# Two attention kinds and a gated MLP on one core: chunks in natural order, and a schedule planner that models shared load bandwidth

## The chip, the cores and the metric

The kernel runs on one core of one Trainium2 chip. The metric is the device time of one execution in microseconds, as the median of several runs. Beside it stands one execution under the hardware profiler, from which the profile's numbers come; its times are microseconds from the start of the span.

## The reference, cut to what matters

Attention over 4 batches of 8 heads, 768 positions of 64 values. Heads 0, 2 and 6 see all earlier positions ("full" heads); the other five see the first 4 positions and a window of 64 ("stream" heads). What comes out, all heads side by side (3072 x 512), goes through two weight matrices with a gate between them.

```
scores = scale * np.matmul(q, k.transpose(0, 1, 3, 2))
stream_keep = causal & (is_sink | in_win)          # 4 sinks, window 64
mask = causal for full heads, stream_keep for the others
a = softmax(scores where mask)
x = (a @ v) with the heads side by side            # 3072 x 512
h = x @ w_in                                       # 512 x 2048
g = h * (1.0 / (1.0 + np.exp(-beta * h)))
out = g @ w_out                                    # 2048 x 512
```

## The kernel before

The work is cut into eight chunks: one batch and one half (384 positions) of its sequence each. For a chunk, four pairs of heads (p and p + 4, one in the upper and one in the lower 64 rows of TensorE) go through scores (task S), exp on ScalarE, a mask, the product with the values (PV), and the division by the row sum on VectorE (rec, x). A chunk that is the second half of its batch also needs the first half's keys and values: a full head has 15 blocks of 128 x 128 scores there instead of 6, a stream head 6 instead of 5. The chunk's x is transposed (Tx on TensorE with an eviction, or Xx by a DMA), and then come 16 groups F1 of four matmuls with w_in (line 701), each followed by a tanh on ScalarE (703) and a gate product on VectorE (705), and 12 groups F2 of four matmuls with w_out (719), whose results are scaled into osb tiles (730, 732) and stored from the SP queue (735). F1.1.3 below is the fourth F1 group of chunk 1; F2.0.0.4 is chunk 0, first 128 rows, gate blocks 4 to 7.

Keys and queries reach TensorE in two ways. In the way of the ramp (`load_pair`, `keys_ramp`) float32 pairs are loaded from SP, cast, transposed by TensorE (Tk, Tq, line 448) and evicted. In the way of rows (`load_rows`, `keys_rows`) GpSimd issues DMAs that cast to bfloat16 (417), twelve to a chunk, and SP issues DMA transposes (462) into KT and QT. Before, chunks 0, 1 and 2 go the first way (`N_F32 = 3`). Values are loaded from SP (`load_v`, 392) into four vs tiles and copied to VX (CV) and, for the stream heads' previous block and sinks, to VO; KO holds the like for keys. The first two chunks add their masks on TensorE (M, line 590); later ones multiply on VectorE. Four PSUM banks are for scores (`S_BANKS`) and four for all else (`G_BANKS`).

The weights come in four parts each, issued by GpSimd. `W_AFTER` names for each part a load that must have landed first: GpSimd copies one element of it (`held`), then issues the DMA.

The order on every engine is written by a planner (`Plan.run`) when the kernel is built. It plays the tasks through with estimated durations and puts each task where its engine is first free; on chip each engine runs its list in that order and waits where an operand isn't there yet. `pick` chooses among tasks that are ready: on TensorE attention always stands ahead of F1 and F2. A transfer's landing is estimated with one common queue:

```
begin = max(dma_free, now + occ + 1000.0)
dma_free = begin + service
t.done = dma_free + 1000.0
```

`fill` puts matmuls on zeros into planned holes of the first 36 us.

Of the kernel before, what the change touches and what calls it, by code (L numbers as in the profile page):

```python
# [16 lines left out]
class Slots:  # L17


    def __init__(self, names, in_turn=False):  # L20
        self.names = list(names)
        self.free = [0.0] * len(self.names)
        self.in_turn, self.holds = in_turn, []
# [5 lines left out]
    def turn(self, hold):  # L29
        if not self.in_turn:  # L30
            return True
        while self.holds and self.holds[0].got is not None:
            self.holds.pop(0)
        return self.holds[0] is hold
# [41 lines left out]
class Plan:  # L76


    SEM = {"PE": 55.0, "ACT": 40.0, "DVE": 38.0, "POOL": 66.0, "SP": 70.0}
    SWITCH = 100.0  # L80

# [10 lines left out]
    def run(self, pick):  # L92
# [7 lines left out]
        def enter(t):  # L100
            for e, occ, lat in t.alts:
                at = max((d.start if e == d.engine == "PE" else d.done + self.SEM[e] for d in t.deps), default=0.0)
                at = max([at] + [d.start for d in t.follow])
                ready[e].append((at, t, occ, lat))
# [5 lines left out]
        dma_free = 0.0  # L110
        lanes = {"hw": [], "sw": []}
        n = len(self.tasks)
        left = n
        while left:
# [72 lines left out]
RAMP_C = 2  # L187
FILL_END, FILL_SPARE = 36000.0, 120.0
N_F32 = 3
W_AFTER = [("v", 0, 0), ("q", 1, 3), ("v", 1, 0), ("v", 1, 2), ("wi", 1), ("wi", 2), ("wo", 0), ("wo", 1)]  # L190
C2_AFTER = ("wi", 2)
V2_AFTER = ("wi", 3)


def XT_PE(c, m):
    return c < 4 or (c == 7 and m % 2)
# [3 lines left out]
def kernel(  # L200
# [24 lines left out]
    chunks = [(b0 + i, h2) for b0 in range(0, B, 2) for h2 in range(2) for i in range(2)]  # L225
# [47 lines left out]
    A7 = sb([128, 5, 128], BF16, "A7")  # L273
    Ac = sb([128, 5, 128], BF16, "Ac")
    junk = sb([1, 64], F32, "junk")
# [49 lines left out]
    t_as = ops("DVE", 100, [lambda: less(A7[:, 0:3], M7[:, 0:3]), lambda: nc.vector.tensor_copy(out=A7[:, 3:5], in_=A7[:, 1:3])], "adds", [t_m, t_m1, t_m2], prio=-24)  # L325
# [18 lines left out]
    seq = [0]  # L344

    def dma(name, queue, issue, service, deps, fn, take=(), drop=(), prio=None, follow=()):
        seq[0] += 1
        kind = "sw" if queue == "POOL" else "hw"
        lat = 0.0
        return P.add(name, [(queue, issue, lat)], deps, seq[0] * 0.001 + (prio or 0), lambda _: fn(eng[queue]), take, drop, land=(kind, service), follow=follow)  # L350
# [45 lines left out]
    def load_w_in(i, key):  # L396
        f = slice(i * 512, (i + 1) * 512)
        t = held(key, lambda: w_in_sb[0:1, 0, i * 512:i * 512 + 1])
# [3 lines left out]
    def load_w_out(i, key):  # L402
        f = slice(i * 4, (i + 1) * 4)
        t = held(key, lambda: w_out_sb[0:1, i * 4, 0:1])
# [5 lines left out]
    def load_rows(c, deps=(), follow=()):  # L410
        b, h2 = chunks[c]
        hold = Hold(stage_r)
        for name, src in (("k", k), ("q", q)):
            i = "kq".index(name)
            for t in range(HT):
                r = h2 * HALF + t * 128
                ROW[name, c, t] = [dma(f"row{name}{c}.{t}.{a}", "POOL", 750, 850, list(deps), lambda e, t=t, a=a, r=r, i=i, src=src: e.dma_start(  # L417
# [38 lines left out]
    def keys_rows(c, deps=()):  # L456
        hold = ROW[c]
        for name, holder, made in (("k", KH, GK), ("q", QH, GQ)):
            i = "kq".index(name)
            ts = []  # L460
            for t in range(HT):
                ts.append(dma(f"X{name}{c}.{t}", "SP", 1250, 650, ROW[name, c, t] + list(deps), lambda e, t=t, i=i, holder=holder: e.dma_start_transpose(
# [5 lines left out]
    def sinks(c):  # L468
# [3 lines left out]
        for p in OP:  # L472
# [8 lines left out]
            for src, lo, hi, at in todo:  # L481
                ts.append(P.add(f"KO{c}.{p}", [dve((hi - lo) * 128, 0.27), pool((hi - lo) * 128)], GK[src, p], c * 100 + 50 + p,
# [3 lines left out]
            t = P.add(f"KOs{c}.{p}", [dve(16), pool(16, 4.0)], ts + GK[f, p], c * 100 + 50 + p,  # L486
# [4 lines left out]
    def values(c):  # L491
# [3 lines left out]
        for t in range(HT):  # L495
            hold = LD["vhold", c, t]
            GV[c].append(P.add(f"CV{c}.{t}", [pool(512, 0.96), dve(512, 0.53)] if c >= 2 else [dve(512, 0.53), act(512, 20)], [LD["v", c, t]], c * 100 + 60,
# [4 lines left out]
        on = (lambda n: [dve(n, 0.27)]) if c < RAMP_C else (lambda n: [pool(n, 0.9), dve(n, 0.27)])  # L502
# [13 lines left out]
    def side_of(c, p, a):  # L516
# [7 lines left out]
        if retr[h]:  # L524
# [14 lines left out]
            return bks, per, [("c", (0, 1))], 16 if h2 else 7  # L539
# [3 lines left out]
        for i in range(HT):  # L543
# [4 lines left out]
            else:  # L548
                at = i - 1 if h2 == 0 else i
                order.append((K(c, i - 1) if c < RAMP_C else KOk(at), VOv(at), i))  # L550
# [10 lines left out]
    def attention(c, p):  # L561
# [13 lines left out]
        for rs in groups:  # L575
# [4 lines left out]
            m_task = []  # L580
            if by_pe:
                def put(_, work=work):
                    for a, r, bank in work:
                        lo, lst = sides[a][0][r]
                        w = sum(n for _, _, n in lst)
                        if sides[a][2][0][0] == "s":
                            add = A7[:, lo:lo + w].rearrange("p k j -> p (k j)")
                        else:
                            add = Ac[:, 2 * r:2 * r + 3].rearrange("p k j -> p (k j)")
                        nc.tensor.matmul(bank.buf[:, 0:add.shape[1]], ident, add, start=True, stop=False)  # L590
                m_task = [P.add(f"M{c}.{p}", [pe(384 * len(work), len(work))], [t_ac, t_as, t_id], prio + 1, put, take=[w[2] for w in work])]

            def go(_, work=work):
# [7 lines left out]
                for r, at, a, kk, q0, n, bank in sorted(todo, key=lambda x: x[:3]):  # L601
                    to, of = bank.buf[:, at * 128:(at + n) * 128], QH[c].buf[half(a), p, q0 * 128:(q0 + n) * 128]
                    nc.tensor.matmul(to, kk(), of, start=not by_pe, stop=(r, at + n) == ends[a, r] or not by_pe)  # L603
                if by_pe:
                    for a, r, bank in work:
                        if sides[a][2][0][0] == "s" and r == 1:
                            nc.tensor.matmul(bank.buf[0:sink_i, 0:128], sink_of(c, a, p), QH[c].buf[half(a), p, 256:384], start=True, stop=True)
# [66 lines left out]
    def x_transposed(c):  # L674
        for m in range(MO):
# [11 lines left out]
            else:  # L687
                XTD[c, m] = dma(f"Xx{c}.{m}", "SP", 1250, 480, deps, lambda e, m=m: e.dma_start_transpose(
# [66 lines left out]
    for i in range(4):  # L755
        load_w_in(i, W_AFTER[i])
# [3 lines left out]
    for i in range(4):  # L760
# [104 lines left out]
```

## Time and profile before

| | before |
|---|---|
| median of 3 runs | 235.78 us (235.77 to 235.97) |
| the profiled execution | 237.91 us, of which span 236.1 us |
| mean granted TensorE clock | 0.993 |
| instructions in the span | 5174 |
| read from and written to memory | 27.27 MB, 6.29 MB |

Busy times are shares of the span. A matmul's end is modelled, so TensorE's busy time is over what it works; the distance between the starts of matmuls is the better price, and a run of equal matmuls in the timeline gives it. In the chain of work that ended last, each step is followed back to what released it.

### The profile page before, as it was taken

To read this page: it belongs to the slowest core of one execution; us is meant where nothing else is said; L and a number is where in the kernel's file an instruction comes from. 1 tells how busy PE (TensorE), PEld (TensorE's weight loads), DVE (VectorE), ACT (ScalarE), POOL (GpSimd) and SP (SyncE) were. 2 spreads that over 40 slices of the span, in tenths; PEclk is the share of its full clock that TensorE was granted. 3 is DMA by queue.
4 is the path that set the end of the run, shared out by engine and by line. 5 is a ranking of instruction groups with operands and counts; after the bars stand their busy time and mean duration, and the time that the engine had idled before them with its cause. 6 is when DMAs were issued, how large, how long until landed. Compare 5 with 4: busy or idle time off the path is not lost.

```text
span 236.1 us, 5174 instructions
## 1 busy us (share of the span) xinstructions
PE 227.0 (96%) x1898; PEld 125.8 (53%) x1898; DVE 147.6 (63%) x350; ACT 157.3 (67%) x339; POOL 75.8 (32%) x152
## 2 busy tenths in 40 slices
PE   7969989989999999999999999999999999999994
PEld 3546565544655545555554554555555555555553
DVE  5874878786857546558983886677756443434320
ACT  2947959797745569749786886889975645555400
POOL 4302431841991781799921334030000000000000
PEclk9997999999999999999999999999999999999999
DMA  6999999999899999999994696472121001111112
GB/s 199 247 212 230 174 172 261 254 176 100 158 168 186 158 199 152 122 193 229 130 174 105 148 131 117 109 149 61 21 78 47 24 22 46 47 44 44 44 47 89
DMA packets 93482, 31.10 MB, mean 132 GB/s; under 512 B 79744, under 2 KB 90512, under 8 KB 93456
## 3 DMA queue, kind: packets, MB, share of 16 engines
q1 hardware_dynamic: 56688, 22.10, 41.3%
q0 software_dynamic: 35904, 8.13, 41.0%
q10 hardware_dynamic: 864, 0.53, 0.7%
q8 instruction: 15, 0.25, 0.5%
q14 instruction: 11, 0.09, 0.1%
HBM read 27.27 MB, written 6.29 MB: 142 GB/s over the span
## 4 chain that ended last, share of the span: by engine, by line
PE 87%; DMA 5%; DVE 3%; SPq 2%; ACT 1%; issue 1%; ACTq 0%
PE bank L719 36%; PE bank L701 35%; PE bank L603 7%; PE bank L663 5%; DMA qs<-in_q_dram 5%; SPq L392 1%; PE bank L448 1%; PE bank L590 1%; PE bank L683 1%; SPq L379 1%; DVE gT L705 1%; DVE x L671 1%; ACT es L615 1%; ACT th L703 0%; DVE qkb L280 0%
## 5 line engine op out<-in xcount | busy, mean ns | idle before, releaser
L703 ACT ACTIVATE th<-bank,beta_h 128x384 f32<-128x384 f32 x128 | 74.4, 585 | 39.6 <-PE bank L701 31.7
L705 DVE SCALAR_TENSOR_TENSOR gT<-th,bank 128x384 bf16<-128x384 f32 x128 | 70.2, 551 | 46.8 <-ACT th L703 42.3
L701 PE MATMUL bank<-xT,w_in_sb 128*128 128x384 bf16 x512 | 95.9, 326 | 0.2 <-ACT xT L280 0.2
L719 PE MATMUL bank<-w_out_sb,gT 128*128 128x512 bf16 (+1 forms) x400 | 96.0, 371 | 0.0
L701 PEld LDWEIGHTS <-w_in_sb 128*128 128x128 bf16 x512 | 48.3, 98 | 37.2 <-issue 1.5
L719 PEld LDWEIGHTS <-gT 128*128 128x128 bf16 x400 | 37.0, 98 | 35.5 <-issue 2.6
L615 ACT ACTIVATE es<-bank 128x384 bf16<-128x384 f32 (+1 forms) x96 | 37.5, 477 | 11.6 <-PE bank L603 11.5
L615 ACT ACTIVATE esL<-bank 128x384 bf16<-128x384 f32 x68 | 28.0, 506 | 1.1 <-PE bank L603 1.0
L280 POOL COPY KO<-KT 128x128 bf16<-128x128 bf16 (+3 forms) x23 | 8.0, 370 | 48.5 <-DVE KO L280 17.8
L603 PE MATMUL bank<-QT,KT 64*128 64x128 bf16 (+2 forms) x258 | 22.9, 252 | 0.3 <-ACT QT L280 0.3
L417 POOL DMA_DIRECT2D qs<-in_q_dram x30 | 22.7, 786 | 0.9 <-issue 0.9
L417 POOL DMA_DIRECT2D ks<-in_k_dram x30 | 22.5, 797 | 0.0
L730 ACT ACTIVATE osb<-bank 128x512 f32<-128x512 f32 (+1 forms) x16 | 8.9, 559 | 13.3 <-DVE osb L732 9.9
L603 PEld LDWEIGHTS <-KT 64*128 64x128 bf16 x258 | 10.5, 95 | 13.3 <-issue 11.6
L671 DVE TENSOR_TENSOR x<-bank,rec 128x384 bf16<-128x384 f32 x32 | 17.3, 550 | 0.4
L630 DVE TENSOR_TENSOR es<-es,M 128x768 bf16<-128x768 bf16 (+1 forms) x24 | 12.5, 529 | 4.9 <-ACT es L615 4.9
L732 DVE TENSOR_SCALAR osb<-bank 128x512 f32<-128x512 f32 (+1 forms) x11 | 6.8, 617 | 10.3 <-PE bank L719 10.3
L667 DVE RECIPROCAL rec<-bank 128x6 f32<-128x6 f32 x32 | 6.0, 191 | 11.3 <-PE bank L663 11.2
L663 PEld LDWEIGHTS <-es 128*128 128x128 bf16 x268 | 10.6, 98 | 3.9 <-issue 0.7
L663 PE MATMUL bank<-VX,es 128*128 128x65 bf16 x200 | 11.6, 195 | 0.2 <-DVE gT L705 0.2
L280 POOL COPY VO<-VX 128x512 bf16<-128x512 bf16 (+2 forms) x7 | 6.0, 860 | 9.1 <-PE bank L603 5.3
L663 PEld LDWEIGHTS <-esL 128*128 128x128 bf16 x204 | 7.0, 97 | 1.1
(76 smaller groups left out, 149.9 us busy)
## 6 DMA issues: line engine op xcount, KB each, us to landing
vs<-in_v_dram SPq DMA_DIRECT2D x24, 256.0 KB, 5.4
out_dram<-osb SPq DMA_DIRECT2D x23, 256.0 KB, 2.2
ks<-in_k_dram SPq DMA_DIRECT2D x12, 192.0 KB, 5.9
w_in_sb<-in_moe_w_in_dram POOLq DMA_DIRECT2D x4, 512.0 KB, 8.0
w_out_sb<-in_moe_w_out_dram POOLq DMA_DIRECT2D x4, 512.0 KB, 9.0
qs<-in_q_dram SPq DMA_DIRECT2D x10, 192.0 KB, 8.6
ks<-in_k_dram POOLq DMA_DIRECT2D x30, 64.0 KB, 5.7
qs<-in_q_dram POOLq DMA_DIRECT2D x30, 64.0 KB, 4.3
```

What stands on the lines that cost most here:

```text
L280: (nc.scalar.copy if e == "ACT" else eng[e].tensor_copy)(out=out, in_=in_)
L417: ROW[name, c, t] = [dma(f"row{name}{c}.{t}.{a}", "POOL", 750, 850, list(deps), lambda e, t=t, a=a, r=r, i=i, src=src: e.dma_start(out=hol ...
L603: nc.tensor.matmul(to, kk(), of, start=not by_pe, stop=(r, at + n) == ends[a, r] or not by_pe)
L615: EX[a].append(P.add(f"exp{c}.{p}", [act(w * 128)], [t], prio, lambda _, a=a, place=place, w=w, bank=bank: nc.scalar.activation(out=es.buf ...
L630: masks.append(P.add(f"mask{c}.{p}", [dve(2 * (hi - lo) * 128, 0.53)], [EX[0][r], EX[1][r], t_mask], prio, lambda _, lo=lo, hi=hi: nc.vect ...
L663: nc.tensor.matmul(view()[:, i, a, 0:D + 1], es.buf[:, (base[a] + at) * 128:(base[a] + at + 1) * 128], val(), start=(j == 0), stop=(j == l ...
L671: nc.vector.tensor_mul(xo, view()[:, :, :, 0:D], rec.buf.to_broadcast([128, HT, 2, D]))
L701: nc.tensor.matmul(bank.buf[:, 0:HALF], w_in_sb[:, mo, fi * 128:(fi + 1) * 128], XTH[c].buf[:, mo, :], start=(mo == 0), stop=(mo == MO - 1))
L703: t = P.add(f"th{c}.{fi}", [act(HALF, 97)], [t, t_beta], c * 100, lambda _, fi=fi, bank=bank, th=th: nc.scalar.activation(out=th.buf, in_= ...
L705: GATE[c, fi] = P.add(f"gate{c}.{fi}", [dve(HALF)], [t], c * 100, lambda _, fi=fi, bank=bank, th=th: nc.vector.scalar_tensor_tensor(out=GH ...
L719: nc.tensor.matmul(bank.buf[:, 0:hi - lo], GH[c].buf[:, fi, ns * 128:(ns + 1) * 128], w_out_sb[:, fi, lo:hi], start=(fi == 0), stop=(fi == ...
L730: nc.scalar.activation(out=osb.buf[:, 0:h - l], in_=src, func=ACTF.Copy, scale=0.5)
```

## The change

- The chunks go in natural order: both halves of batch 0, then of batch 1 and so on. Before, the first halves of two batches came first and then their second halves. So the second chunk of the ramp is now a second half.
- Chunk 2 now goes by rows and DMA transposes as chunks 3 to 7 do; x is transposed on TensorE for chunks 0 and 1 alone (and half of chunk 7).
- GpSimd's DMAs have an order of their own (`SW_ORDER`): each starts after the one ahead of it has been issued. Only the first two parts of w_in wait for a landing; chunk 2's rows stand between w_in and w_out.
- For a full head in a second half the 15 blocks lie in four banks (4, 4, 4, 3 blocks) instead of five (3 each), so in two rounds instead of three; the masks that TensorE adds in the ramp are widened to fit.
- GpSimd copies no values, KO or VO tiles any more; VectorE does.
- The planner plays its plan through eight times (`PLANNED`). After each round it works out when the loads land if the queues that have work share the bandwidth (`landings`), and uses half of the correction in the next. What waits for a landing is planned 100 ns later.
- On TensorE attention has no absolute precedence any more: behind chunk 2 it is ordered among F1 and F2 as if due 1.5 chunks (`LEAD`, 24 groups of F1) before its own F1.

```
-    chunks = [(b0 + i, h2) for b0 in range(0, B, 2) for h2 in range(2) for i in range(2)]
+    chunks = [(i, h2) for i in range(B) for h2 in range(2)]
...
-W_AFTER = [("v", 0, 0), ("q", 1, 3), ("v", 1, 0), ("v", 1, 2), ("wi", 1), ("wi", 2), ("wo", 0), ("wo", 1)]
+SW_ORDER = ["i0", "i1", "i2", "i3", 2, "o0", "o1", "o2", "o3"]
+W_AFTER = {"i0": ("v", 0, 0), "i1": ("q", 1, 3)}
...
-    return c < 4 or (c == 7 and m % 2)
+    return c < 2 or (c == 7 and m % 2)
...
+    def landings(self):
...
+            step = min(min(queues[q][0][1] for q in live) * len(live), nxt - now)
+            now += step
+            for q in live:
+                at, left, t = queues[q][0]
+                left -= step / len(live)
...
+    def run(self, pick, rounds=1):
...
+            self.once(pick, lag)
+            out = self.landings()
...
+                    lag[t.seq] = new if t.seq not in lag else 0.5 * (new + lag[t.seq])
...
-                begin = max(dma_free, now + occ + 1000.0)
-                dma_free = begin + service
-                t.done = dma_free + 1000.0
+                t.done = now + occ + lag.get(t.seq, self.BEFORE + service + self.BEHIND + 500.0)
...
-            bks.append((0, bank(0, [(d, 1, 1, 2), (d, 2, 2, 1)])))
-            bks.append((4, bank(4, [(d, 0, 0, 3)])))
+            what = {0: [(d, 1, 1, 2), (d, 2, 2, 1)], 4: [(d, 0, 0, 3)]}
             if h2:
-                for j in range(HT):
-                    bks.append((7 + 3 * j, bank(7 + 3 * j, [(f, j, 0, 3)])))
+                what[0].append((f, 0, 0, 1))
+                what[4].append((f, 0, 1, 1))
+                what[8] = [(f, 0, 2, 1), (f, 1, 0, 3)]
+                what[12] = [(f, 2, 0, 3)]
...
-            GV[c].append(P.add(f"CV{c}.{t}", [pool(512, 0.96), dve(512, 0.53)] if c >= 2 else [dve(512, 0.53), act(512, 20)], ...
+            GV[c].append(P.add(f"CV{c}.{t}", [dve(512, 0.53)] if c >= 2 else [dve(512, 0.53), act(512, 20)], ...
...
-                    return (1, i if kind == "F1" else i * 16.0 / 12.0 + F2_LAG, x[1].seq)
-                return (0, pr, x[1].seq)
+                    return (i if kind == "F1" else i * 16.0 / 12.0 + F2_LAG, x[1].seq)
+                c, rest = divmod(pr, 100)
+                return ((c - LEAD) * 16.0 + rest * 0.32 if c > 2 else pr - 1000.0, x[1].seq)
```

More of the change, by code (lines that the diff above doesn't have):

```diff
@@ new lines, in run @@
+    def run(self, pick, rounds=1):
+        lag = {}
+        best = None
+        for i in range(rounds):
+            self.reset()
+            self.once(pick, lag)
+            out = self.landings()
+            off = max(abs(out[t.seq] - t.done) for t in self.order if t.land is not None and t.seq in out)
+            late = sum(max(0.0, out[t.seq] - t.done) for t in self.order if t.land is not None and t.seq in out)
+            self.log = getattr(self, "log", []) + [(self.end, off, late)]
+            for t in self.order:
+                if t.land is not None:
+                    new = out[t.seq] - t.start - t.alts[0][1]
+                    lag[t.seq] = new if t.seq not in lag else 0.5 * (new + lag[t.seq])
+        return self.order
@@ L93, in run, with once @@
+    def once(self, pick, lag):
         free = dict.fromkeys(self.SEM, 0.0)
@@ L580, in attention, with added @@
             m_task = []
+            def added(a, r):
+                return by_pe and (sides[a][2][0][0] == "s" or r < 2)
             if by_pe:
@@ L827 @@
     P.fill = fill
-    for t in P.run(pick):
+    for t in P.run(pick, PLANNED):
         t.emit(t.engine)
```

138 lines of the change are left out of this document (86 added, 52 removed).

## The prediction

> **What bounds the kernel now.** I read the page first (shares, slices, chain), then TensorE in order of time, stretches cut at the point where it stops waiting, and at last ScalarE's, GpSimd's and the transfers' rows.
>
> ```profile
> span 236.1 us, 5174 instructions
> PE 227.0 (96%) x1898; PEld 125.8 (53%) x1898; DVE 147.6 (63%) x350; ACT 157.3 (67%) x339; POOL 75.8 (32%) x152
> PE   7969989989999999999999999999999999999994
> PEclk9997999999999999999999999999999999999999
> ...
> PE 87%; DMA 5%; DVE 3%; SPq 2%; ACT 1%; issue 1%; ACTq 0%
> PE bank L719 36%; PE bank L701 35%; PE bank L603 7%; PE bank L663 5%; DMA qs<-in_q_dram 5%; SPq L392 1%; PE bank L448 1%; PE bank L590 1%; PE bank L683 1%; SPq L379 1%; DVE gT L705 1%; DVE x L671 1%; ACT es L615 1%; ACT th L703 0%; DVE qkb L280 0%
> ...
> L703 ACT ACTIVATE th<-bank,beta_h 128x384 f32<-128x384 f32 x128 | 74.4, 585 | 39.6 <-PE bank L701 31.7
> ```
>
> TensorE carries 87% of the chain, 71% in the two products of the second half (L701, called F1 here, and L719, F2); no other engine is over 67% busy. Only the first slices have holes and a lower clock. TensorE in order of time there, then ScalarE, then stretches (columns: length, then busy us of PE, PEld, DVE, ACT, POOL; granted clock, DMA share, GB/s):
>
> ```profile
> 15.03 0.72 PE L683 MATMUL bank<-idb,x 128*128 128x128 bf16 x6
> 18.27 0.41 PE L590 MATMUL bank<-Ac,idb 128*128 128x384 bf16 x1 [2.53 <-ACT es L615]
> ...
> 23.66 0.82 PE L701 MATMUL bank<-xT,w_in_sb 128*128 128x384 bf16 x4
> ...
> 33.66 2.60 PE L701 MATMUL bank<-xT,w_in_sb 128*128 128x384 bf16 x15
> ```
>
> ```profile
> 7.65 1.53 ACT L615 ACTIVATE es<-bank 128x384 bf16<-128x384 f32 x4 [0.27 <-PE bank L603]
> ...
> 17.43 0.51 ACT L280 CAST qkb<-qs 128x384 bf16<-128x384 f32 x1 [2.31 <-DMA qs<-in_q_dram]
> 17.84 0.65 ACT L615 ACTIVATE es<-bank 128x256 bf16<-128x256 f32 x2
> ...
> 20.73 0.51 ACT L280 CAST qkb<-qs 128x384 bf16<-128x384 f32 x1 [0.75 <-DMA qs<-in_q_dram]
> ```
>
> ```profile
> 18.20:21.80 3.60, 3.53 (x34) 2.73 (x34) 1.60 (x4) 2.25 (x7) 0.23 (x1) 0.53 1.01 248
> 5.46:36.91 31.45, 27.80 (x315) 17.34 (x313) 23.06 (x60) 23.54 (x58) 8.47 (x22) 0.95 1.08 211
> 36.91:232.90 195.99, 194.98 (x1573) 106.72 (x1571) 121.44 (x274) 132.01 (x279) 64.59 (x114) 1.00 0.81 119
> ```
>
> The worst wait, 2.53 us, is one of order: the exps that free TensorE's banks stand on ScalarE behind a cast that waits 2.31 us for a query load. Right after it TensorE runs at 0.53 of its clock for 3.6 us, some 1.7 us of work lost. From 33.66 it runs without a break; its eleventh F1 group (F1.0.10, four matmuls to a group) starts five groups later, at 36.91. I cut there: what lies behind is 195.99 us with 1.0 us idle shown, so it shrinks only by TensorE work taken out.
>
> **The change, part by part.** Prices of TensorE's work, in order of time, merged by the chain or the timeline:
>
> ```profile
> 182.70 1.95 PE bank L701 x12
> 184.65 0.86 PE bank L719 x4
> ...
> 62.39 2.00 PE bank L663 x63
> ```
>
> ```profile
> 47.87 0.27 PE L603 MATMUL bank<-QT,KT 64*128 64x256 bf16 x1 [0.31 <-ACT QT L280]
> ...
> 48.34 0.68 PE L448 MATMUL bank<-idb,qkb 128*128 128x128 bf16 x9
> 49.62 0.33 PE L448 MATMUL bank<-idb,qkb 128*128 128x128 bf16 x3 [0.25 <-DVE QT L280]
> ...
> 52.38 1.03 PE L719 MATMUL bank<-w_out_sb,gT 128*128 128x512 bf16 x4
> 53.34 0.23 PE L603 MATMUL bank<-QT,KO 64*128 64x128 bf16 x2
> ...
> 53.57 0.22 PE L603 MATMUL bank<-QT,KO 64*128 64x128 bf16 x2
> 53.63 0.22 PE L603 MATMUL bank<-QT,KT 64*128 64x128 bf16 x2
> 53.78 1.04 PE L719 MATMUL bank<-w_out_sb,gT 128*128 128x512 bf16 x4
> ```
>
> An F1 group is 0.65 us, an F2 group 0.86, a value matmul (L663) 0.031, a transpose about 0.057 (nine in 0.68 with a last one of 0.22), a pair of score blocks (both heads at once) 0.056. Before a run of scores the F2 group takes 0.96 (52.38 to 53.34) instead of 0.86, and the last block 0.15 instead of 0.06: each run of scores costs 0.19 us for entering and leaving.
>
> Behind F1.0.10 the built program has, against before:
> - 24 fewer key and query transposes (chunk 2 now comes in as bf16 rows, turned by DMA): 24 x 0.057 = 1.4. The 0.31 and 0.25 us waits beside them go too: 0.6.
> - 24 fewer x transposes (chunks 2 and 3 by DMA): 1.4.
> - one second half less and one first half more, as chunk 1, in the ramp, is now a second half: 32 blocks, 16 pairs x 0.056 = 0.9, and 32 value matmuls x 0.031 = 1.0.
> - 30 runs of scores instead of 38 (four full banks per head, two rounds instead of three; fewer second halves): 8 x 0.19 = 1.5.
>
> Sum: 6.2 of work and 0.6 of waits. F1, F2 and the last 10 us are the same.
>
> Ahead of F1.0.10, TensorE's extra work for chunk 1 is 0.9 + 1.0, four more runs (0.8) and wider mask matmuls (0.5): 3.2 us. Against it: the exps of pair 3 no longer stand behind the second query cast but behind the first, which had landed, so the 2.53 us wait and its slow clock may go. The load order of chunks 0 and 1 is unchanged. Query group 1.2 lands at 20.73; its cast, three transposes, the masks and one run for pair 1.1 bring the first F1 to 22.0 (23.66 before). From there to F1.0.10 stand: ten F1 groups 6.5, 24 score pairs 1.35, seven runs 1.3, ten mask matmuls (six at an F1 matmul's 0.163, four of 512 columns at an F2 matmul's 0.216) 1.85, 75 value matmuls 2.3, 18 transposes 1.0: 14.3 us, so 36.3 at the earliest. ScalarE, at 0.36 us an exp of 384 columns (four in 1.53) and some 0.46 for 512 (an estimate from it), has 8.8 us of exps, ten tanhs of 0.6 and six copies of 0.4 (17.43 to 17.84) from 17.43: free by 34.6. Two engines that near alternate rather than overlap fully; I put F1.0.10 at 38.0, 1.1 late, between 36.3 and 36.91 + 3.2 = 40.1.
>
> The new route of chunk 2 and of the weights is what could hold TensorE. GpSimd's and the transfers' rows (the lines with three figures: least, median, most):
>
> ```profile
> 22.33 0.74 POOL L399 DMA_DIRECT2D w_in_sb<-in_moe_w_in_dram  x1 [0.31 <-POOL w_in_sb L368]
> ...
> 28.65 0.29 POOL L368 COPY w_out_sb<-w_in_sb 1x1 bf16<-1x1 bf16 x1 [2.45 <-DMA w_in_sb<-in_moe_w_in_dram]
> 33.83 0.41 POOL L368 CAST vs<-w_in_sb 1x1 f32<-1x1 bf16 x3 [1.29 <-DMA w_in_sb<-in_moe_w_in_dram]
> 43.33 4.55 POOL L417 DMA_DIRECT2D ks<-in_k_dram  x6
> ...
> L417 POOL DMA_DIRECT2D ks<-in_k_dram x6: 750/766/868, 43.3 to 47.0; - x6
> DMA to landing us min/median/max: 5.8/9.6/11.0
> ...
> L462 SPq DMA_TRANSPOSE QT<-qs x15: 1188/1196/2707, 68.2 to 150.0; - x15
> DMA to landing us min/median/max: 2.4/4.1/8.9
> ```
>
> The last three w_in loads now go out back to back, then twelve row loads, then w_out. w_in lands at 28.65 and by 33.83 as before; F1.0.4 needs the first and comes at about 29. TensorE reaches F2.0.0.0 after 18 more F1 groups: 38.0 + 11.7 = 49.7, and the scores of chunk 2 (S2.0) at 50.6. Fast end: rows issued at 0.77 us each from 22.33 + 3 x 0.75 = 24.6 to 33.8, landed 5.8 later at 39.6, the last tile turned 1.2 + 2.4 later: 43.2. Slow end: issued only from 33.83 to 43.1, landed at 54.1, turned in 2.7 + 8.9: 65.7. I take the medians with the early issue, as GpSimd stands idle by then: 33.8 + 9.6 + 1.2 + 4.1 = 48.7, 1.9 under the cover of 50.6. F2.0.0.0 needs the first w_out, issued behind the rows and landing up to 11.0 later, at 44.8 to 54.1: a wait of 4.4 us at the worst. For all new waits I take 0.5 us. The copies of values (CV, VO) and of keys (KO) leave GpSimd for VectorE (groups kept apart by shape: total and mean ns; then SP's longest wait):
>
> ```profile
> L280 DVE CAST VX<-vs 128x512 bf16<-128x512 f32 x14 | 6.2, 448 | 0.1
> L280 DVE COPY KO<-KT 128x128 bf16<-128x128 bf16 x9 | 1.7, 222 | 0.1
> ```
>
> ```profile
> SPq L735 <- ACT osb L730: 52.3, 12, 7.0
> ```
>
> 37 more copies of 0.22 to 0.45 us, about 11 us, and 10 casts and evictions of 0.45 fewer: 6 us net on an engine busy 121 of 196 us. It is free unless a copy that waits for a transfer stands ahead of the gate products that free F1's banks: in the built program the KO copies of chunks 2 and 3 stand ahead of the third gate of chunk 1, at about 45, and chunk 2's value casts ahead of its last ones. SP gets 14 more transposes of 1.2 us (6 of keys and queries, 8 of x), 17 us, in order with the stores and value loads; it has 52.3 us of waiting for output tiles alone to put them in, so they cost nothing while the next consumer is further off than that order.
>
> One row speaks for this and a rule against: an issue of a row load takes 0.75 to 0.87 us while VectorE is busy. The Trainium skill, SBUF — State Buffer, section "SBUF: two separate sides", says that a DMA issued by GpSimd finds its descriptor writing locked out while VectorE runs an operation in a mode that uses two ports. By that rule the added copies stretch the issues. The trace agrees with 0.1 us of it at most.
>
> **Sum.** Span 236.1 - 6.2 - 0.6 + 1.1 + 0.5 = 230.9. The profiled execution took 237.91 us, span and 1.8 around it; the median of the runs, 235.78, is 0.3 under the span. Unchanged ends, so the forecast is 235.78 - 5.2 = 230.6.
>
> **Rivals.**
> - The ramp gives nothing back (chance 0.17): ScalarE becomes its bound, or the slow clock falls again, and F1.0.10 comes at 40.1: 235.78 - 6.8 + 3.2 + 0.5 = 232.7. For it: ScalarE's 3.5 us of additional exps and its share of 23.54 of 31.45 us. Against: three of its casts and copies go. The Trainium skill, TensorE: Matmul & The Clock Gate, section "What's actually happening", has the clock halve after an idle window of about 3.4 us; the trace shows the halving after 2.5 us of idling, and once more would be the 1.7 us above.
> - Slower (chance 0.13): chunk 2 comes late. TensorE works in program order, and behind S2.0 stand the rest of F1.1, all of F2 and the next chunks. Each us after 50.6 costs one; it decides from 50.6 + 5.2 = 55.8, and the slow end, 65.7, gives 245.7. w_out, queued behind the same rows, adds to it. Of its chance 0.02 is for issues stretched by a whole copy of VectorE, 0.77 + 0.45 = 1.22 us, which move the slow end to 71.1 and the time to 251.1. For it: 9.6 us median landing in the neighbouring row. Against: GpSimd has no copies to wait for any more.
> - More than forecast (0.06): all 1.0 us of idle behind the cut goes and F1.0.10 comes at 36.3: 235.78 - 6.2 - 1.0 - 0.6 = 228.0.
> - It does nothing (0.02): the ramp at 40.1 and 3.6 of those 4.4 us of waiting for w_out cancel the gain, 235.8.
>
> **The numbers.** The forecast itself has 0.62. The range 227.6 to 235.2 leaves out the slower rival, the null case and a little of both ends. About 0.2%, 0.5 us, is what the measurement can tell from no change: faster by more 0.84, within 0.02, slower 0.14 (the slower rival and a last piece of the ramp's upper bound with late w_out).
>
> **What would show it.** Right: no 2.5 us wait on an exp before 18.3; first F1 near 22; F1.0.10 near 38; 48 transposes at the L448 line's successor and 30 of x; TensorE at nine tenths in all slices behind 38. Wrong: F1.0.10 after 40.1; a wait of TensorE at S2.0 or F2.0.0.0 on a transfer or on KO; gate products idle behind a value cast; the issues of rows clearly over 0.87 us.

## The result, and the profile after

The changed kernel takes 252.14 us (median; 251.9 to 254.63), the kernel before 235.88 us beside it: a ratio of 1.0682 [1.0576, 1.0787]. The forecast was 230.6 us, at most 235.2. Medians are of all runs; ratios compare the means of the runs that a lower clock did not disturb, so they can differ a little from the quotient of the medians.

The page of the changed kernel (span and its instructions; busy share of TensorE and its clock in 40 slices; shares of the chain that ended last):

```profile
span 250.1 us, 5103 instructions
PE 227.0 (91%) x1863; PEld 124.7 (50%) x1887; DVE 150.6 (60%) x378; ACT 149.3 (60%) x313; POOL 64.2 (26%) x116
PE   7999999729599999989998599599999999999994
PEclk9999999985999999999999979999999999999999
...
PE 66%; DMA 16%; DVE 5%; SPq 4%; issue 3%; ACT 2%; POOL 2%; DVEq 0%; ACTq 0%; POOLq 0%
PE bank L776 26%; PE bank L794 24%; DMA vs<-in_v_dram 13%; PE bank L738 5%; PE bank L674 4%; SPq L453 3%; PE bank L660 2%; PE bank L397 2%; DMA xT<-x 2%; DVE gT L780 1%; DVE VX L337 1%; POOL qs L478 1%; DMA out_dram<-osb 1%; PE bank L509 1%
```

TensorE fell from 87% to 66% of the chain; the loads of values (vs, 13%), absent from before's chain, are now its third item. The slices have no hole in the ramp and several behind it. TensorE in order of time, at the points that the prediction named and at its first stops (in brackets: idle time ahead, and what ended it):

```profile
21.41 0.82 PE L776 MATMUL bank<-xT,w_in_sb 128*128 128x384 bf16 x4
...
36.74 7.96 PE L776 MATMUL bank<-xT,w_in_sb 128*128 128x384 bf16 x48 [0.34 <-DVE gT L780]
46.52 4.08 PE L776 MATMUL bank<-xT,w_in_sb 128*128 128x384 bf16 x24 [1.83 <-DVE gT L780]
...
56.31 0.80 PE L674 MATMUL bank<-QT,KT 64*128 64x256 bf16 x6 [4.83 <-DMA QT<-qs]
...
66.32 0.43 PE L738 MATMUL bank<-VX,es 128*128 128x65 bf16 x9 [2.46 <-DVE gT L780]
```

First F1 at 21.41, F1.0.10 at 36.74, then waits: for gate products, and 4.83 us for a query tile of chunk 2. I also reckoned both traces by the distances between the starts of TensorE's matmuls, every distance beyond the undisturbed price of its kind counted as loss. Taken as recorded, work fell from 214.3 to 206.2 us, loss rose from 12.4 to 32.9, and fills and ends took the rest of the 14.0 by which the span grew. But the trace of the changed kernel lacks 23 F2 matmuls whose weight loads it has (before's has all 400):

```profile
L794 PE MATMUL bank<-w_out_sb,gT 128*128 128x512 bf16 (+1 forms) x377 | 92.6, 375 | 1.7 <-issue 0.8
L794 PEld LDWEIGHTS <-gT 128*128 128x128 bf16 x400 | 37.8, 99 | 37.0 <-issue 3.2
```

At 0.216 us each (an F2 group of 0.86 has four) they are 5.0 us of work that stands among the loss. So work fell by some 3 us and loss rose by some 15.5; other prices of a matmul move both by a little over 1 us. Part of the loss is TensorE's clock: by an estimate from mean clock and span, what was not granted comes to 5.5 us after (0.978 over 250.1 us) and 1.7 before (0.993 over 236.1).

The stage 20 to 65 us, before and then after (columns as in the prediction's windows; the DMA share sums the times of packets, so it can pass 1):

```profile
20.00:65.00 45.00, 43.52 (x408) 25.18 (x406) 35.17 (x83) 36.12 (x81) 21.16 (x42) 0.98 1.14 185
```

```profile
20.00:65.00 45.00, 36.81 (x321) 20.15 (x321) 26.78 (x66) 30.40 (x64) 25.78 (x42) 0.92 1.51 160
```

The 16 transfer engines work a third longer and move less: 160 GB/s, not 185. The transfers of this stage, before (queues with their share; issues with KB and median us to landing) and after:

```profile
q0 software_dynamic: 9625, 4.41, 76.9%
...
w_out_sb<-in_moe_w_out_dram POOLq DMA_DIRECT2D x4, 512.0 KB, 9.0
vs<-in_v_dram SPq DMA_DIRECT2D x6, 256.0 KB, 9.4
```

```profile
q0 software_dynamic: 16113, 5.21, 117.3%
...
w_out_sb<-in_moe_w_out_dram POOLq DMA_DIRECT2D x4, 512.0 KB, 14.2
...
vs<-in_v_dram SPq DMA_DIRECT2D x3, 256.0 KB, 12.9
...
QT<-qs SPq DMA_TRANSPOSE x3, 13.0
```

GpSimd's queue carries 6488 packets more; the time of its packets, summed and divided by 16, rises from 34.6 to 52.8 us (76.9% and 117.3% of the 45). A part of w_out takes 14.2 us to land, not 9.0, and values take 12.9, not 9.4; query transposes land after 13.0 us. SP's queue after:

```profile
32.81 4.24 SPq L523 DMA_TRANSPOSE KT<-ks  x3
37.23 8.16 SPq L523 DMA_TRANSPOSE QT<-qs  x3
45.50 10.51 SPq L453 DMA_DIRECT2D vs<-in_v_dram  x3
69.33 2.49 SPq L763 DMA_TRANSPOSE xT<-x  x2
71.92 1.21 SPq L523 DMA_TRANSPOSE KT<-ks  x1
```

Chunk 2's six transposes stand ahead of its values, which go out at 45.50; before, the like loads went out at 38.99. SP had stood 13.1 us, from 19.7 to 32.8, at the first of these transposes, for a key row of chunk 2; behind the values it stands 14.0 us at an x transpose. VectorE, and behind it the chain around 45 to 66 us (start, length, what):

```profile
45.61 0.40 DVE L337 COPY KO<-KT 128x128 bf16<-128x128 bf16 x3 [2.00 <-DMA KT<-ks]
...
46.60 4.56 DVE L780 SCALAR_TENSOR_TENSOR gT<-th,bank 128x384 bf16<-128x384 f32 x8
58.47 0.43 DVE L337 CAST VX<-vs 128x512 bf16<-128x512 f32 x1 [7.30 <-DMA vs<-in_v_dram]
58.81 0.55 DVE L780 SCALAR_TENSOR_TENSOR gT<-th,bank 128x384 bf16<-128x384 f32 x1
```

```profile
46.13 6.17 SPq L453
...
52.39 12.23 DMA vs<-in_v_dram
...
64.72 0.49 DVE VX L337
...
65.81 0.47 DVE gT L780
66.28 0.04 issue
66.32 0.49 PE bank L738 x11
```

Read downwards this is the mechanism: a value load goes out only when the one ahead of it, 6.17 us in issuing, is through, and takes 12.23 to land; it holds a cast; the gate product that stands behind the cast on VectorE holds a bank; TensorE waits for the bank.

### The profile page after: what moved, and what is told of

The parts are those of the page before. It is cut to its first block, busy times and chain, and to the rows that moved or that the text cites. A ratio compares the mean times of both kernels' runs of the same rounds, so it can differ in the third digit from the quotient of the medians.

```text
span 250.1 us, 5103 instructions
## 1 busy us (share of the span) xinstructions
PE 227.0 (91%) x1863; PEld 124.7 (50%) x1887; DVE 150.6 (60%) x378; ACT 149.3 (60%) x313; POOL 64.2 (26%) x116
## 4 chain that ended last, share of the span: by engine, by line
PE 66%; DMA 16%; DVE 5%; SPq 4%; issue 3%; ACT 2%; POOL 2%; DVEq 0%; ACTq 0%; POOLq 0%
PE bank L776 26%; PE bank L794 24%; DMA vs<-in_v_dram 13%; PE bank L738 5%; PE bank L674 4%; SPq L453 3%; PE bank L660 2%; PE bank L397 2%; DMA xT<-x 2%; DVE gT L780 1%; DVE VX L337 1%; POOL qs L478 1%; DMA out_dram<-osb 1%; PE bank L509 1%; ACT th L778 1%
## 5 line engine op out<-in xcount | busy, mean ns | idle before, releaser
L776 PE MATMUL bank<-xT,w_in_sb 128*128 128x384 bf16 x512 | 97.1, 329 | 5.5 <-DVE gT L780 4.8
L794 PE MATMUL bank<-w_out_sb,gT 128*128 128x512 bf16 (+1 forms) x377 | 92.6, 375 | 1.7 <-issue 0.8
L794 PEld LDWEIGHTS <-gT 128*128 128x128 bf16 x400 | 37.8, 99 | 37.0 <-issue 3.2
L478 POOL DMA_DIRECT2D ks<-in_k_dram x36 | 27.1, 776 | 19.0 <-DMA KT<-ks 11.0
L478 POOL DMA_DIRECT2D qs<-in_q_dram x36 | 27.1, 774 | 12.4 <-DMA w_out_sb<-in_moe_w_out_dram 5.3
L690 ACT ACTIVATE esL<-bank 128x512 bf16<-128x512 f32 (+1 forms) x56 | 27.5, 578 | 3.3 <-PE bank L674 3.3
L337 DVE CAST VX<-vs 128x512 bf16<-128x512 f32 x24 | 10.8, 449 | 21.5 <-DMA vs<-in_v_dram 21.5
L738 PE MATMUL bank<-VX,esL 128*128 128x65 bf16 x192 | 8.2, 201 | 3.0 <-DVE gT L780 3.0
L452 POOL MEMSET vs<- 128x1 f32 x18 | 2.0, 140 | 33.5 <-DVE VX L337 33.5
L738 PEld LDWEIGHTS <-esL 128*128 128x128 bf16 x204 | 7.8, 102 | 4.5 <-issue 3.2
## 6 DMA issues: line engine op xcount, KB each, us to landing
w_out_sb<-in_moe_w_out_dram POOLq DMA_DIRECT2D x4, 512.0 KB, 14.2
```

The source lines that it names most:

```text
L337: (nc.scalar.copy if e == "ACT" else eng[e].tensor_copy)(out=out, in_=in_)
L690: EX[a].append(P.add(f"exp{c}.{p}", [act(w * 128)], [t], prio, lambda _, a=a, place=place, w=w, bank=bank: nc.scalar.activation(out=es.buf ...
L738: nc.tensor.matmul(view()[:, i, a, 0:D + 1], es.buf[:, (base[a] + at) * 128:(base[a] + at + 1) * 128], val(), start=(j == 0), stop=(j == l ...
L776: nc.tensor.matmul(bank.buf[:, 0:HALF], w_in_sb[:, mo, fi * 128:(fi + 1) * 128], XTH[c].buf[:, mo, :], start=(mo == 0), stop=(mo == MO - 1))
L794: nc.tensor.matmul(bank.buf[:, 0:hi - lo], GH[c].buf[:, fi, ns * 128:(ns + 1) * 128], w_out_sb[:, fi, lo:hi], start=(fi == 0), stop=(fi == ...
```

## The experiments

The edits have letters, as several were combined; a letter puts a part back as it was before. All ratios are to the kernel before, run beside. GpSimd's fixed order of DMAs stays in all kernels made from after. "Held" means as in `W_AFTER` before.

| label | made from | edits | us | ratio |
|---|---|---|---|---|
| b2_four_banks | before | four banks | 236.9 | 0.999 [0.9953, 1.0028] |
| b1_rows_chunk2 | before | chunk 2 by rows | 244.5 | 1.03 [1.0238, 1.0363] |
| e9_values_elsewhere | after | spare tiles for values | 244.12 | 1.0286 [1.0223, 1.0348] |
| e1_pool_copies | after | G | 247.48 | 1.0431 [1.0353, 1.0509] |
| e2_margin | after | margin 6000 ns | 255.1 | 1.0666 [1.0564, 1.0769] |
| e3_old_landing | after | L | 251.59 | 1.0615 [1.0532, 1.0698] |
| e10_x_transposes_pe | after | X | 258.37 | 1.0877 [1.0809, 1.0944] |
| e4_attention_first | after | A | 251.4 | 246.63 to 252.78 us |
| e14_weights_held | after | W | 249.06 | 1.0493 [1.0411, 1.0575] |
| e6_chunk2_pairs | after | P | 243.73 | 1.0273 [1.0214, 1.0332] |
| e7_pairs_old_landing | after | P L | 244.4 | 1.0315 [1.0257, 1.0373] |
| e15_pairs_weights_held | after | P W | 251.13 | 1.0589 [1.0517, 1.0661] |
| e11_pairs_xt_pool | after | P X G | 244.09 | 1.0278 [1.0236, 1.0321] |
| e12_order_banks_weights | after | P X G L A | 241.4 | 1.019 [1.0132, 1.0249] |
| e13_order_banks | after | P X G L A W | 238.51 | 1.0056 [1.0022, 1.009] |
| e17_order_banks_pick | after | P X G L W | 238.86 | 1.0063 [1.0015, 1.011] |
| e18_order_banks_planner | after | P X G A W | 251.17 | 1.0615 [1.0502, 1.0728] |
| e16_planner_pick_left | after | P X G W | 244.78 | 1.0309 [1.0214, 1.0404] |

**Do late values hold TensorE through VectorE?** e9_values_elsewhere keeps the order and all transfers, but no cast waits for a load.

```
-            out=hold.buf, in_=v[b, :, r:r + 128, :]
+            out=hold.buf if c < 2 else spare[t], in_=v[b, :, r:r + 128, :]
```

> The order of every engine and every transfer stay those of the changed kernel, but the value loads of chunks 2 to 7 land in three spare tiles, and the value copies (CV) of these chunks read what the first two chunks left, so their output is not the reference's. Only CV's wait for a landing is gone. Theory A (value copies that wait for their loads stand on VectorE ahead of gate products and so hold F1's and PV's banks): TensorE's waits on gate products (5.4 + 4.8 us) and the half clock after them go, and with them the row loads that wait behind the vs memsets come earlier; 252.1 falls to 234 to 241. Rival B (transfers have too much to move until 65 us, whatever waits for them): TensorE then waits for keys and queries instead, 248 or more.

244.12: 8.0 us off, between the two ranges expected. So about half of the loss went through casts that wait. The run does not tell why the values were late.

**G: copies may go to GpSimd again.** e1_pool_copies:

```
-    [dve(512, 0.53)] if c >= 2 else
+    [pool(512, 0.96), dve(512, 0.53)] if c >= 2 else
...
-    on = lambda n: [dve(n, 0.27)]
+    on = (lambda n: [dve(n, 0.27)]) if c < RAMP_C else (lambda n: [pool(n, 0.9), dve(n, 0.27)])
```

> The value, VO and KO copies may go to GpSimd again as before; all else is the changed kernel. Theory A (what matters is that they stand ahead of gates on VectorE): part of them goes, 238 to 247; what GpSimd then waits for, it waits for ahead of its row loads. Rival B: 248 or more.

247.48, 4.7 us off and just outside the range for it: VectorE's copies weren't free. TensorE's waits for query transposes stayed at 4.8 us in all.

**Is the planner's landing estimate too early?** e2_margin plans all that waits for a landing 5.9 us later still; L, in e3_old_landing, goes back to the estimate with a common queue, its old durations, no margin and one round.

```
-MARGIN = 1000.0, 1000.0, 100.0
+MARGIN = 1000.0, 1000.0, 6000.0
```

> One number: the planner puts whatever waits for a landing 6 us instead of 0.1 us behind the landing that it computes (MARGIN 100 to 6000). Theory A with the planner's landings too early as its root (values of chunk 2 planned to land at 46.5 to 50.8, landed at 58.5 to 64.7): copies move behind more gate products, 234 to 244. Rival B: nothing is moved sooner by it, 248 to 256.

```
-PLANNED = 8
+PLANNED = 1
...
-                t.done = now + occ + lag.get(t.seq, self.BEFORE + service + self.BEHIND + 500.0)
+                begin = max(dma_free, now + occ + 1000.0)
+                dma_free = begin + service
+                t.done = dma_free + 1000.0
```

> The planner's part alone undone: one round, one common queue for all landings with the old services (850 ns a row load, 650 and 480 a transpose), no margin; natural order, row route of chunk 2, four banks and VectorE copies stay. Theory A with its root in the landing model: 230 to 241. Rival B (the changed traffic itself, twelve row loads and six transposes instead of eight pair loads for chunk 2 in a stage where the transfers are full): 246 or more.

255.1 and 251.59: no gain, so at this point the estimate looked acquitted. e3's trace shows that it wasn't, quite. VectorE's waits for values (in all, times, longest), after and e3:

```profile
DVE VX L337 <- DMA vs<-in_v_dram: 21.5, 9, 7.3
```

```profile
DVE VX L340 <- DMA vs<-in_v_dram: 2.2, 2, 1.3
```

The casts no longer stood ahead of their loads; yet something else cost as much. I took it to be the transfers themselves, and undid those.

**P: chunk 2 by float32 pairs again.** e6_chunk2_pairs:

```
-SW_ORDER = ["i0", "i1", "i2", "i3", 2, "o0", "o1", "o2", "o3"]
+SW_ORDER = ["i0", "i1", "i2", "i3", "o0", "o1", "o2", "o3"]
...
+    for p in range(NP):
+        for x in "kq":
+            load_pair(2, p, x, deps=[gate[x]], prio=15)
+        keys_ramp(2, p)
```

> The changed kernel with chunk 2's keys and queries by the way of before: float32 pairs from SP behind the third part of w_in, cast and transposed on TensorE (1.4 us of work more there); its values behind the fourth. Theory D (the transfers from 20 to 65 us bound the middle: packets there took 67.6 us of the 16 engines against 51 before, and chunk 2's twelve row loads and six DMA transposes are the difference): TensorE's wait at S2.0 and the value waits up to 65 us go, 234 to 241. Rival A2 (copies on VectorE and the ordered GpSimd queue alone hold the gates, whatever the traffic): 246 or more.

243.73, 8.4 us off, between the two ranges expected. b1_rows_chunk2 does the opposite to the kernel before:

```
-N_F32 = 3
+N_F32 = 2
...
-load_rows(c, follow=[LD["wo", 3]])
+load_rows(c, follow=[LD["wi", 3] if c == 2 else LD["wo", 3]])
```

> The kernel before with one part of the change: chunk 2 by rows behind the fourth part of w_in, instead of float32 pairs; all else as before. Theory D: slower by 4 to 14 us, 240 to 250. Rival A2: the copies still go to GpSimd, so no more than 1 us either way, 234 to 237.

244.5, 7.3 us on. Its stage 20 to 65 us, and SP's waits at its transposes (total, times, longest); before had 6.1 in three, the longest 2.8:

```profile
20.00:65.00 45.00, 40.62 (x300) 22.95 (x297) 30.34 (x69) 29.53 (x61) 24.35 (x42) 0.92 1.47 166
```

```profile
SPq L462 <- DMA ks<-in_k_dram: 22.8, 2, 13.9
SPq L462 <- DMA w_out_sb<-in_moe_w_out_dram: 7.4, 1, 7.4
```

With the old planner and the old everything else the rows alone bring the transfer share from 1.14 to 1.47, and SP stands 13.9 us with its queue behind it. So the rows are one sufficient cause; whether the time is lost through the fuller transfers or through SP's standing, b1 does not separate.

**X: x of chunks 2 and 3 on TensorE**, alone, and with P and G:

```
-    return c < 2 or (c == 7 and m % 2)
+    return c < 4 or (c == 7 and m % 2)
```

> The changed kernel with x of chunks 2 and 3 transposed on TensorE again (1.4 us of work there, eight DMA transposes fewer). Theory D: the eight stand at 69 us and later, behind the worst stage; 248 to 253. A theory E, that the x transposes on SP hold the row transposes and values behind them (they wait 15.4 us for gates and 14.0 for exps there): 240 to 247.

> Three parts undone at once: chunk 2 by float32 pairs, x of chunks 2 and 3 on TensorE, copies allowed on GpSimd. What is left of the change: natural order, four banks, order of the weights, planner. If the parts left are good by themselves (206 us of useful work on TensorE plus 2.8 put back, against 214): 229 to 235. If the natural order or the planner itself brings the waits: 240 or more.

258.37, worse by 6 us, and 244.09, no better than P alone. Taking transposes from the transfers does not pay by itself; why it cost 6 us, outside both ranges expected, I did not settle.

**What is left without rows?** e7_pairs_old_landing is P and L; e12 adds X, G and A (attention first on TensorE, as before); e13 adds W, the held weights, and leaves natural order and the four banks.

```
-                    return (i if kind == "F1" else i * 16.0 / 12.0 + F2_LAG, x[1].seq)
-                c, rest = divmod(pr, 100)
-                return ((c - LEAD) * 16.0 + rest * 0.32 if c > 2 else pr - 1000.0, x[1].seq)
+                    return (1, i if kind == "F1" else i * 16.0 / 12.0 + F2_LAG, x[1].seq)
+                return (0, pr, x[1].seq)
...
-W_AFTER = {"i0": ("v", 0, 0), "i1": ("q", 1, 3)}
+W_AFTER = {"i0": ("v", 0, 0), "i1": ("q", 1, 3), "i2": ("v", 1, 0), "i3": ("v", 1, 2), "o0": ("wi", 1), "o1": ("wi", 2), "o2": ("wo", 0), "o3": ("wo", 1)}
```

> Chunk 2 by float32 pairs and, with it, the planner's landings as before: one round, one common queue, the old services, no margin. In the run with pairs alone TensorE waited at 36 to 52 us for casts that wait for their loads (2.4 + 0.9 + 1.0 us, and as much unseen). Theory P (what the traffic leaves of the loss is the planner's landings, too early for full queues): 232 to 239. Rival N (the natural order or the new order of attention on TensorE makes the waits): 242 or more.

> Left of the change: natural order with a second half in the ramp, four banks, the order of the weight loads. Undone: row route of chunk 2, x transposes by DMA, copies on VectorE alone, planner's landings, order of attention on TensorE. Theory P: 230 to 237. Rival N (natural order makes the waits): 242 or more. A rival W (weights unheld fill the queues ahead of chunk 2's pairs and values): 238 to 243, and less when they are held again.

> As the one with order, banks and weights, but each weight part waits again for the landing that it waited for before. Left: natural order with a second half in the ramp, and four banks. By the prediction's own prices it should do 216 us of useful work instead of 214 plus 1.5 fewer for runs of scores: 231 to 236 under P and W, 242 or more under N.

244.4, 241.4, 238.51. The first lies in the range of rival N, the natural order, but the last refutes it: order and banks leave 0.56%, where my steps had a gain. X, G and A together give 3.0 us; in e7 one KO copy on VectorE still waits 6.1 us for a key transpose and TensorE 5.1 us for a query transpose. Between the last two runs only the weights differ: not holding them costs 2.9 us there. b2_four_banks is the banks alone, in the kernel before:

```
-                    bks.append((7 + 3 * j, bank(7 + 3 * j, [(f, j, 0, 3)])))
+                what[8] = [(f, 0, 2, 1), (f, 1, 0, 3)]
+                what[12] = [(f, 2, 0, 3)]
```

> The kernel before with four banks of 512 columns for the full heads of second halves alone: eight runs of scores fewer at 0.19 us and twelve exps fewer. By the prediction's price 1.5 us faster, 233.5 to 235.5; if the planner's order shifts for the worse with it, 236 to 240.

236.9, within 0.3% up and 0.5% down of before: the 1.5 us are not there (at most 1.1 are). It is the best of the variants, and no proven gain.

**Do weights and rows add up?** W alone in the changed kernel, and P with W:

> The changed kernel with one thing undone: the last two parts of w_in and all of w_out wait for the landings that they waited for before. Chunk 2's rows, the planner and the order on TensorE stay. Transfer theory: pairs and rows cost about 8 of the 15 us and unheld weights about 3, and the two add up; so some 249, and the wait of the first scores of chunk 2 for a query tile stays or grows, since its rows now stand behind held weights (up to 256). Rival: the weights and the rows harm the same transfers, and whichever comes first is enough; then 244 or less. If holding the weights does nothing (251 to 252), the 3 us measured elsewhere belong to another order of the plan.

> The changed kernel with chunk 2 by float32 pairs, as before, and the weights held as before. Left of the change: natural order, four banks, the planner's rounds, TensorE's order, VectorE's copies, x of chunks 2 and 3 by DMA. Transfer theory: 243.7 of the pairs alone less about 3, 240 to 241. Rival, the planner or TensorE's order make the rest by themselves: 243 to 244, with waits of TensorE for gate products left.

249.06 as expected, but 251.13 against 240 to 241: with chunk 2's transfers and all weights as before, 7.4 us slower than P alone. Neither theory had that. The transfers' amount was not the whole cause; what was left was the planner and TensorE's order.

**Planner or TensorE's order?** From e13, the changed planner and order together (e16), the order alone (e17, without A), the planner alone (e18, without L). A alone in the changed kernel is e4.

> The changed kernel with before's order on TensorE: attention always ahead of F1 and F2. Theory that TensorE's order is no cause: 250 to 253, perhaps worse, as scores of chunk 2 are put still further ahead of their tiles. Rival, that the later attention lets the buffers of rows and values come free later and so delays the transfers: 246 or less.

> As the kernel with natural order and four banks alone (238.5), but with the changed planner and the changed order on TensorE; pairs, held weights, x of chunks 2 and 3 on TensorE and copies on GpSimd as before. If planner and order on TensorE cost something by themselves it stands over 238.5 by that: 240 to 241 if they make the 2.7 us that the step from 244.1 to 241.4 showed. If that step came from the planner's answer to early weights alone, 238 to 239.

> Natural order, four banks and the changed order on TensorE; the planner's landings, the weights' holds, chunk 2's pairs, x of chunks 2 and 3 on TensorE and GpSimd's copies are before's. It stands to 238.5 (order and banks) as TensorE's order alone does, and to 244.8 (the same with the changed planner) as the planner does. If TensorE's order makes the 6.3 us between these two: 244 to 246. If the planner's landings make them: 238 to 239.5.

> The counterpart: natural order, four banks and the changed planner (shared bandwidth, eight rounds), with before's order on TensorE, attention first. If the planner's landings make the 6.3 us: 244 to 246, with VectorE's casts of values waiting for landings that the plan has earlier than they come. If TensorE's order makes them: 238 to 239.5. If neither reaches 241 alone, the two only harm together.

With the old landings TensorE's order does nothing (238.86 against 238.51). With the new ones it does: the planner with before's order takes 251.17, with the changed order 244.78. So the planner costs 12.7 us in the one case (e13 to e18) and 5.9 in the other (e17 to e16); neither e16 nor e18 is within the range expected. e4 ranges from 246.63 to 252.78 and settles nothing. e13 and e18 move the same 93 thousand packets. The chains that ended last in e13 and in e18 (9 points of the second one's DMA are loads of values):

```profile
PE 83%; DMA 5%; DVE 4%; ACT 2%; SPq 2%; issue 2%; ACTq 0%
```

```profile
PE 57%; DMA 19%; DVE 10%; SPq 8%; issue 2%; ACT 1%; POOL 1%; ACTq 0%; DVEq 0%; POOLq 0%
```

Waits for values on VectorE, then of SP at its transposes, in e13 and in e18:

```profile
DVE VX L340 <- DMA vs<-in_v_dram: 0.4, 1, 0.4
...
SPq L526 <- DMA ks<-in_k_dram: 4.3, 3, 2.0
```

```profile
DVE VX L337 <- DMA vs<-in_v_dram: 10.2, 8, 3.0
...
SPq L523 <- DMA ks<-in_k_dram: 16.6, 2, 15.4
```

The new lists put casts and transposes ahead of transfers that haven't landed, and both queues stand with work behind. The plans, played again from the kernels' sources, agree: of the value loads that land between 35 and 140 us, the median one lands 2.1 us ahead of the plan in e13, 7.6 us behind it in e18 and 13.8 us behind it in the changed kernel. Part of that lateness follows from the waits themselves. VectorE's waits for values separate the planners: 6.7 to 26.9 us in all in kernels with the new landings (e9 aside, whose casts wait for none), 2.2 at most in those with the old ones. They do not rank the times: e3 has 2.2 and takes 251.59.

So two causes are each enough by themselves: the planner's landings (238.51 to 251.17, from order and banks) and chunk 2 by rows (237.2 to 244.5 on the kernel before; 244.4 to 251.59 from e7 to e3, with old landings). Their prices don't add up. The planner's is 12.7 or 5.9 us there, but 0.6 in the changed kernel (e3), and none beside chunk 2 by pairs (e6 243.73, e7 244.4). That each makes the same queues stand is my reading of it, not shown.

Nor are these two all of it. With both undone e7 still stands 7.2 us over the kernel before; X, G and A then give 3.0, held weights 2.9, and order and banks keep 1.4. Holding the weights gives some 3 us in two places (e12 to e13, after to e14), shows nothing clear in a third (e11 to e16) and costs 7.4 in a fourth (e6 to e15). A price that is measured in one plan is not the price in another, as the planner writes the lists anew after each edit. In eight of the 18 experiments the time fell outside the ranges expected (e9, e1, e6, e10, e13, e15, e16, e18). Left open: which part of the planner (shared bandwidth, half corrections, the new durations, the margin; I undid them together), and why e15 is 7.4 us over e6. The plans differ there throughout.

## Why the prediction was wrong, point by point

**"For all new waits I take 0.5 us": the term that failed.** TensorE's loss rose by some 15.5 us instead. The steps that led there follow.

**The ramp: right.** No 2.5 us wait, first F1 at 21.41 (22.0), F1.0.10 at 36.74 (38.0), so the cautious 1.1 us weren't needed.

**Work removed: held.** It fell by some 3 us over the whole span by the reckoning above, and my steps give 6.2 behind the cut less 3.2 added in the ramp, 3.0. The transposes are there as counted:

```profile
L509 PE MATMUL bank<-idb,qkb 128*128 128x128 bf16 x48 | 4.7, 233 | 0.0
...
L758 PE MATMUL bank<-idb,x 128*128 128x128 bf16 x30 | 2.7, 219 | 0.0
```

It was no gain, since the loss grew by more. The four banks' 1.5 us did not show when tried alone.

**"33.8 + 9.6 + 1.2 + 4.1 = 48.7": the step that failed first.** The rows were in time: their issues ended at 35.91, two us later than the 33.8 (GpSimd waited 2.42 and 1.79 us for parts of w_in to land), but the last one landed at 43.01, where the sum has 43.4. The last term was not. SP's transposes of chunk 2 (least, median, most ns; first and last start; then us to landing):

```profile
L523 SPq DMA_TRANSPOSE KT<-ks x3: 1206/1294/1523, 32.8 to 35.8; - x3
L523 SPq DMA_TRANSPOSE QT<-qs x3: 1632/1977/2252, 37.2 to 43.1; - x3
...
DMA to landing us min/median/max: 4.6/10.9/13.4
```

The last query transpose went out at 43.14, as soon as its row was there, and landed 13.03 us later, at 56.17, not after 4.1; S2.0 began at 56.31. I took medians from a stage with a DMA share of 0.81 for one at 1.1, to which the change adds transfers. The share stood in my own windows (1.01 and 1.08), and I budgeted no transfer time.

**"They cost nothing" of SP's 14 transposes: wrong.** The 52.3 us of waiting that I had for cover are spread over the whole span; the six of chunk 2 keep SP from 32.81 to 45.39, some 9.9 us of it in issuing, ahead of its value loads, which left 6.5 us later than the like before.

**"Free unless a copy that waits for a transfer stands ahead of gate products".** The condition held, and I had seen it in the built order; I gave it no price. The first wait is where I had put it: a KO copy waits 2.00 us at 45.61, and TensorE 1.83 us at 46.52 behind the next gate product. Without waits for values the kernel is 8.0 us faster (e9); with copies allowed on GpSimd, 4.7 (e1).

**The slower rival: right place, price too small.** S2.0 came at 56.31, just past its 55.8, which by one for one would be about no change. The rest is what stands behind: from 60 us on TensorE lost some 15 us by the reckoning above (2.7 before), at values and rows of the next chunks. Its chance, 0.13, and the upper end suffered from the same missing budget.

**The planner: not priced at all.** I read its lists as given. That its casts and transposes stand ahead of landings which come later costs 12.7 us where it is the only edit (e13 to e18), 5.9 with the changed order on TensorE, and 0.6 where the rows stay (e3). So how much of the 16 us is its part stays open.

**w_out** took 14.2 us to land, but TensorE did not wait for it: F2 began at 50.45 (49.7).

**SBUF rule.** Rows were issued in 742 to 896 ns with VectorE's copies added, 745 to 868 before: no stretch, as taken. Another rule bears on the case. The Trainium skill, DMA: Bandwidth & Descriptors, section "Issuing engines are not separate DMA queues", says that transfers started by different engines run interleaved on the same 16 DMA engines. The trace agrees: beside GpSimd's rows and weights SP's query transposes of chunk 2 landed after 13.0 us (median), and in b1, where the rows are the only edit, after 9.5, against a median of 4.1 in the kernel before, where they came later.

## What to carry to other kernels

Before a load is moved to another route, budget the transfer engines for the stage that it lands in: where their share is near 1, take no median landing from a quieter stage, and count issues on the queue in front of the next load. In a list written out ahead, a landing that is estimated too early holds all that stands behind the waiting instruction; look there for casts ahead of gate products and transposes ahead of loads. When undoing one suspect gives nothing, put each suspect alone into the kernel before: of two sufficient causes one may show nothing when it is removed. And where a planner writes the lists anew after each edit, a price holds for that plan alone.

## What the hardware showed unexpectedly

- Three value loads took SP 10.51 us to issue (45.50), one of them 6.17, though the profile shows no wait between them; before, 10.36 us. Elsewhere single ones took 0.39 us (120.84) and 0.53 (145.68).
- Rows cast on the way are dear: in b1, where they are the only edit, the packets of the stage rose from 18772 to 23731, the transfer share from 1.14 to 1.47, and the rate fell from 185 to 166 GB/s.
- TensorE's clock. A wait of 4.83 us (at 56.31) was followed by 0.50 of the clock until 61.80, waits of 2.46 us (at 66.32) and 2.62 us (at 159.09) by the full clock, one of 2.26 us (at 143.70) by 0.55; before, 2.53 us had brought the halving. So a wait of 2.3 to 2.6 us may or may not cost the 1.7 us that I had put on it:

```profile
56.30:60.00 3.70, 3.69 (x16) 1.49 (x16) 0.89 (x2) 1.53 (x4) 2.24 (x4) 0.50 1.61 160
60.00:61.80 1.80, 1.80 (x14) 0.73 (x13) 0.62 (x3) 0.71 (x2) 0.73 (x1) 0.50 1.91 165
...
66.00:70.00 4.00, 3.62 (x42) 2.00 (x43) 2.94 (x8) 1.43 (x4) 4.00 (x6) 1.00 1.54 98
...
143.70:147.50 3.80, 3.80 (x38) 2.71 (x38) 3.22 (x14) 0.58 (x1) 0.10 (x1) 0.55 0.79 140
```
